# Tail transposes issued at once, ScalarE's casts kept behind a pair's second exponential, in the last turns of a fused attention and gated-linear kernel

## The chip, the cores and the metric

The kernel runs on one core of one Trainium2 chip. The metric is the device time of one execution, in microseconds. Five engines work side by side: TensorE (PE in the profile, its weight loads as PEld), VectorE (DVE), ScalarE (ACT), GpSimd (POOL) and SyncE (SP), which issues the transfers. Each engine takes its own instructions in the order in which the program lists them, and semaphores order the engines among each other.

## The reference

```python
x = A_x                                     # 1 x 2048 x 512
g = sigmoid((x * gate_w).sum(-1, keepdims=True))
# A: 32 heads of 16, causal, window 256
q, k, v = split(x @ wqkv)
s = (q @ k.T) * 16 ** -0.5                  # masked to 0 <= i - j < 256
a = (softmax(s) @ v) @ wo
# B: F = 1376
b = (sigmoid(x @ w_gate) * (x @ w_up)) @ w_down
return g * a + (1 - g) * b
```

All tensors are float32. Most matmuls are done in a rounded format three times over, as high part times high part, high times low and low times high, so that a "split" of a tile is a ScalarE cast (the high part) followed by a VectorE subtraction (the low part).

## The kernel before

**Stages.** The sequence of 2048 is cut into 16 blocks of 128 and the heads into 8 groups of 4. A prologue loads and splits x and projects the first values, queries and keys. Then one long loop runs over `u` from 0 to 139. A turn `u` handles one block of one head group for the scores (`s_part`, TensorE into the PSUM tile `s`, then a VectorE reduction to row maxima, L321) and, nine turns later, for the transposed scores (`st_part`, TensorE into `st`, then ScalarE's exponential into `pt`, L366). GpSimd masks `pt`, and every second turn TensorE multiplies two such blocks with the values into `pv` (L394). `s` and `st` have two PSUM banks each. After the loop comes the down projection (tiles `pd`, `hb`) with the output projection (`pa`).

**Fill work.** Between the score matmuls of each head `hh`, the loop puts matmuls of other products: projections of later head groups, the gate and up products (`gu`), and at the end 16 tail groups (`tp`), each of which holds what is left of F and the gate vector for one block of 128 positions. The generator `turns()` hands them out in portions of three steps, and each step is two matmuls on the two row halves of TensorE, where the second half runs 18 steps behind the first. So a group of 12 steps takes 30 steps from its first to its last matmul, and three groups are open in the three banks of the tag `misc`. When a group has ended, its bank must be emptied before the group three later can start: `gu` and projections by a ScalarE copy, tail groups by `tail_post`, a VectorE transpose (L525), a one-column copy (L526), and an entry in `later` for the store to `tail_scratch`.

**The order of the small work.** It is set by hand with two lists. `acts` holds closures that issue ScalarE work, and one is taken per head after the exponential; `behind` holds the VectorE work that follows them, and one is taken per head just before. `acts` gets the emptying of a finished group (put first), the copy of `pv` to `ob` (`o_take`, L410, put first, whose clearing of `pv`, L411, goes first into `behind`), and the splits of weights: `split_d` (L121, low part L122) and `wo_split` (L634, L635). `later` is sent on SyncE's queue at the start of the next turn.

**The last turns.** The scores end with u = 127, and the transposed scores go on to u = 136. From u = 128 on, the portions come in pairs, at the second and the fourth head of a turn. So TensorE does two `st` tiles, twelve `tp` matmuls, two `st` tiles, twelve `tp` matmuls in a turn, and `pv` at the start of each even turn. Here "pair" is two `st` tiles and the twelve matmuls behind them. Below, a pair's exponentials are called first and second.

```python
if t >= SHIFT and (t - SHIFT) % k3 == k3 - 1:          # L623, in turns()
    _, after, post = groups[(t - SHIFT) // k3]
    acts.insert(0, lambda after=after, post=post: (post(), after()))
...
    if behind:                                         # L792, per head
        behind.pop(0)()
    if acts:
        acts.pop(0)()
```

Of the kernel before, what the change touches and what calls it, by code (L numbers as in the profile page):

```python
# [24 lines left out]
NB = T // P  # L25
# [30 lines left out]
def gated_mix_kernel(  # L56
# [49 lines left out]
    NU = NG * NB  # L106
# [22 lines left out]
    with ExitStack() as actx:  # L129
# [175 lines left out]
        def s_part(u, hh):  # L305
            g, i = divmod(u, NB)
            s = g * NC + i // 4
            if i % 4 == 0 and hh == 0:
                mxs[s] = spool.tile([P, HG, 4], F32, tag="mx", name=f"mx{s}")
            k0 = max(0, i - 2)  # L310
            tag = "st" if u < LAG and hh >= 2 else "s"
            pt = ps.tile([P, 3 * P], F32, tag=tag, name=f"s{u}_{hh}", bufs=2)
            lhsT = blk(g, i, hh, 0)
            for k, e in pieces(g, k0, i + 1):
                mm(  # L315
                    pt[:, (k - k0) * P:(e - k0) * P], lhsT, blk(g, k, hh, 1, e - k),
                    start=k == k0, stop=e == i + 1, skip_group_check=True,
                )
            n = (i + 1 - k0) * P
            junk = spool.tile([P, 3 * P], F32, tag="junk", name=f"junk{u}_{hh}", bufs=1)  # L320
            nc.vector.tensor_tensor_reduce(  # L321
                junk[:, 0:n], pt[:, 0:n], mask[:, 3 * P - n:], scale=1.0, scalar=NEG,
                op0=ALU.add, op1=ALU.max, accum_out=mxs[s][:, hh, i % 4:i % 4 + 1],
            )
# [28 lines left out]
        def st_part(u, hh):  # L353
            g, j = divmod(u, NB)
            if u not in pts:
                pts[u] = ppool.tile([P, HG, 3 * P], F32, tag="pt", name=f"pt{u}", bufs=3)
            pt = ps.tile([P, 3 * P], F32, tag="st", name=f"st{u}_{hh}", bufs=2)
            lhsT = blk(g, j, hh, 1)
            last = min(NB, j + 3)
            for q, e in pieces(g, j, last):  # L360
                mm(  # L361
                    pt[:, (q - j) * P:(e - j) * P], lhsT, blk(g, q, hh, 0, e - q),
                    start=q == j, stop=e == last, skip_group_check=True,
                )
            n = (last - j) * P
            nc.scalar.activation(pts[u][:, hh, 0:n], pt[:, 0:n], AF.Exp, scale=SCALE)  # L366
# [15 lines left out]
        acts = []  # L382
        obs = {}

        def pv_part(u):
            g, j = divmod(u, NB)
            p = pts.pop(u)
            last = min(NB, j + 3)
            q = j
            while q < last:  # L390
                e = min(last, (q // 4 + 1) * 4)
                for hh in range(HG):
                    h = g * HG + hh
                    mm(  # L394
                        pv[32 * hh:32 * hh + 32, (q % 4) * P:(q % 4 + e - q) * P],
                        V[:, j, h * VW:h * VW + 32],
                        p[:, hh, (q - j) * P:(e - j) * P],
                        start=False, stop=True, skip_group_check=True,
                        tile_position=(0, 32 * hh),
                    )  # L400
                q = e
            if j % 2 == 1:
                acts.insert(0, lambda: o_take(g * NC + j // 4, j // 2 % 2))
# [71 lines left out]
        def gu_mm(f, c, w, k, half=None):  # L475
            if (f, c, w) not in gp:
                gp[f, c, w] = ps.tile([P, CH], F32, tag="misc", name=f"gu{f}_{c}_{w}", bufs=3)
            group_mm(gp[f, c, w], gv[:, 0, w], gv[:, 1, w], c, k, half)
# [35 lines left out]
        def tail_mm(b, k, half=None):  # L514
            if b not in tp:
                tp[b] = ps.tile([P, CH], F32, tag="misc", name=f"tp{b}", bufs=3)
            d, w = divmod(k, 3)
            r = slice(0, P) if half is None else slice(64 * half, 64 * half + 64)
            mm(tp[b][:, 0:TW], (xl if w == 1 else xh)[r, d, b * P:(b + 1) * P], tw[d][int(w == 2)][r, 0:TW],  # L519
               start=k == 0 and half != 1, stop=k == 3 * ND - 1 and half != 0,  # L520
               skip_group_check=half is not None)

        def tail_post(b):
            t = cpool.tile([P, CH], F32, tag="sp", name=f"tt{b}", bufs=4)
            nc.vector.transpose(t[:, 0:2 * TF], tp[b][:, 0:2 * TF])  # L525
            nc.vector.tensor_copy(gsum[:, b:b + 1], tp.pop(b)[:, 2 * TF:2 * TF + 1])  # L526
            later.append((tail_d[b], t[:, 0:2 * TF]))
# [38 lines left out]
        def proj_slot(s, k, half):  # L566
            g, c = divmod(s, NC)
            d, w = divmod(k, 2) if k < 2 * ND else (k - 2 * ND, 2)
            r = slice(64 * half, 64 * half + 64)
            mm(pair_of_banks(f"ph{s}")[half], wq[g][int(w == 2)][r, d], (xl if w == 1 else xh)[r, d, c * CH:(c + 1) * CH],  # L570
               start=k == 0, stop=k == 3 * ND - 1)

        def proj_sum(s):
            lower, upper = halves.pop(f"ph{s}")
            t = cpool.tile([P, CH], F32, tag="sp", name=f"psum{s}", bufs=4)
            nc.scalar.copy(t, lower)
            pj[s] = t
            behind.append(lambda: nc.vector.tensor_tensor(t, upper, t, op=ALU.add))
            soon.append(lambda: proj_post(s))
# [6 lines left out]
                lambda k, h=None, a=(f, c, w): gu_mm(*a, k, h),  # L586
# [2 lines left out]
            )  # L589
            for f in range(NFM) for w in range(2) for c in range(NC)  # L590
        ] + [
            (lambda k, h=None, b=b: tail_mm(b, k, h), lambda: None, lambda b=b: tail_post(b)) for b in range(NB)
        ]
        work = []
        going = []
# [4 lines left out]
        def run_first(n):  # L600
            for _ in range(n):
                if not going:
                    going.append([0, *(work or first).pop(0)])
                k, step, post = going[0]
                for half in range(2):
                    step(k, half)
                going[0][0] += 1
                if k + 1 == 3 * ND:
                    going.clear()
                    post()  # L610

        def turns():
            k3 = 3 * ND
            groups = []
            for t in range(n_rest * k3 + SHIFT):
                if t and t % GAP == 0:
                    yield
                if t % k3 == 0 and len(groups) < n_rest:
                    groups.append((work or rest).pop(0))
                for half, v in enumerate((t, t - SHIFT)):  # L620
                    if 0 <= v < n_rest * k3:
                        groups[v // k3][0](v % k3, half)
                if t >= SHIFT and (t - SHIFT) % k3 == k3 - 1:  # L623
                    _, after, post = groups[(t - SHIFT) // k3]
                    acts.insert(0, lambda after=after, post=post: (post(), after()))

        def slot(h, d, c):
            return (xh, xl)[h][:, d, c * CH:(c + 1) * CH]
# [8 lines left out]
        def flush(acts):  # L637
            while acts:
                acts.pop(0)()
# [86 lines left out]
        HLOAD = N - 2 * AHEAD  # L726
        done = 0
        slots = turns()
        sdma = []
        wo_raw = []  # L730

        for u in range(N):
# [35 lines left out]
            if s4 is not None:  # L768
                if u < LAG:
                    first.insert(0, (  # L770
                        lambda k, h, s4=s4: proj_slot(s4, k, h), lambda s4=s4: proj_sum(s4)))
# [4 lines left out]
            for hh in range(HG):  # L776
                if hh == 0 and u % 2 == 0:
                    for w in (u - PVLAG - 1, u - PVLAG):
                        if 0 <= w < NU:
                            pv_part(w)  # L780
                if u < NU:
                    s_part(u, hh)
                if 0 <= u - LAG < NU:
                    st_part(u - LAG, hh ^ 1 if u < NU else hh)
                if u < LAG:
                    flush(behind)
                    if hh % 2 == 1:
                        upto = n_first * (2 * u + 1 + hh // 2) // (2 * LAG)
                        run_first(upto - done)
                        done = upto  # L790
                else:
                    if behind:  # L792
                        behind.pop(0)()
                    if acts:
                        acts.pop(0)()
                if u >= LAG and (hh < HG - 1 or u % 2 == 0 if u < NU else hh % 2 == 1):
                    next(slots, None)
                    if u >= NU:
                        next(slots, None)
# [87 lines left out]
        for n, (c, f) in enumerate(steps):  # L887
# [42 lines left out]
            for t in range(4):  # L930
                b = 4 * c + t
# [60 lines left out]
```

## Time and profile before

| | |
|---|---|
| time, median of 3 runs | 745.94 us (745.91 to 746.12) |
| span of the profiled execution | 743.8 us |
| TensorE busy | 737.1 us (99%) |
| VectorE, ScalarE, GpSimd busy | 504.5, 432.3, 171.7 us |
| mean granted TensorE clock | 0.999 |
| tail groups' matmuls | from 507.4 to 576 us of the span |
| turns u = 128 to 137 | about 532.6 to 570 us |

The profile page gives the span of the profiled execution; its own time is not listed beside it, and the three timed runs lie 2.1 us above the span. Times inside the trace are counted from the span's start. In a row of the timeline stand start, duration, engine, line, operation, output<-inputs, shape and count, and in brackets how long the engine had been idle and what ended that. A matmul's end is modelled, so its starts say more than its duration.

### The profile page before, as it was taken

To read this page: it belongs to the slowest core of one execution; us is meant where nothing else is said; L and a number is where in the kernel's file an instruction comes from. 1 tells how busy PE (TensorE), PEld (TensorE's weight loads), DVE (VectorE), ACT (ScalarE), POOL (GpSimd) and SP (SyncE) were. 2 spreads that over 40 slices of the span, in tenths; PEclk is the share of its full clock that TensorE was granted. 3 is DMA by queue.
4 is the path that set the end of the run, shared out by engine and by line. 5 is a ranking of instruction groups with operands and counts; after the bars stand their busy time and mean duration, and the time that the engine had idled before them with its cause. 6 is when DMAs were issued, how large, how long until landed. Compare 5 with 4: busy or idle time off the path is not lost.

```text
span 743.8 us, 17724 instructions
## 1 busy us (share of the span) xinstructions
PE 737.1 (99%) x6310; PEld 585.2 (79%) x6310; DVE 504.5 (68%) x1518; ACT 432.3 (58%) x921; POOL 171.7 (23%) x256
## 2 busy tenths in 40 slices
PE   8999999999999999999999999999999999999997
PEld 7888777887777877778787787778777878787886
DVE  5368767766776766776677676677745685848573
ACT  6423676666676667666667666766655573625341
POOL 7000333233233233323323333232331000000000
PEclk9999999999999999999999999999999999999999
DMA  8341434435434453443543426553367878869561
GB/s 302 102 115 34 103 97 118 127 91 160 125 103 119 120 152 109 120 113 110 153 117 99 126 69 174 151 144 116 92 239 206 233 190 212 196 169 227 148 136 58
DMA packets 94321, 103.66 MB, mean 139 GB/s; under 512 B 44926, under 2 KB 57214, under 8 KB 94232
## 3 DMA queue, kind: packets, MB, share of 16 engines
q1 hardware_dynamic: 94232, 102.53, 49.9%
q8 instruction: 49, 0.80, 0.5%
q14 instruction: 40, 0.33, 0.2%
HBM read 45.32 MB, written 31.99 MB: 104 GB/s over the span
## 4 chain that ended last, share of the span: by engine, by line
PE 97%; DVE 1%; DMA 1%; issue 0%; ACT 0%; SPq 0%; POOL 0%; DVEq 0%; POOLq 0%
PE gu L247 28%; PE pv L394 12%; PE pj L247 11%; PE s L315 7%; PE st L361 5%; PE tp L519 5%; PE pd L78 5%; PE pd L80 5%; PE pd L79 5%; PE vh L556 3%; PE pa L78 2%; PE pa L79 2%; PE pa L80 2%; PE vps L79 1%; PE vps L78 1%; PE vps L80 1%
## 5 line engine op out<-in xcount | busy, mean ns | idle before, releaser
L321 DVE CUSTOM_DVE_ANT_0 junk<-s,mask 128x384 f32<-128x384 f32 (+2 forms) x512 | 271.8, 531 | 126.3 <-PE s L315 69.7
L366 ACT ACTIVATE pt<-st 128x384 f32<-128x384 f32 (+2 forms) x512 | 241.6, 474 | 169.9 <-PE st L361 65.3
L247 PE MATMUL gu<-xh,w 64*128 64x512 f32 x1152 | 295.1, 392 | 0.0
L247 PE MATMUL gu<-xl,w 64*128 64x512 f32 x576 | 190.5, 392 | 0.0
L371 POOL TENSOR_SCALAR_AFFINE_SELECT pt<-pt 128x512 f32<-128x512 f32 x128 | 87.7, 685 | 377.2 <-ACT pt L366 377.2
L247 PEld LDWEIGHTS gu<-xh,w 64*128 64x128 f32 x1152 | 160.6, 184 | 14.1
L361 PE MATMUL st<-ring 64*128 64x384 f32 (+2 forms) x536 | 170.1, 332 | 0.2 <-ACT pt L366 0.2
L315 PE MATMUL s<-ring 64*128 64x384 f32 (+2 forms) x536 | 166.6, 329 | 0.4 <-DVE mx L321 0.4
L315 PEld LDWEIGHTS s<-ring 64*128 64x128 f32 x536 | 95.3, 184 | 37.3 <-DVE nm L331 12.5
L361 PEld LDWEIGHTS st<-ring 64*128 64x128 f32 x536 | 97.0, 184 | 11.2 <-issue 2.7
L247 PEld LDWEIGHTS gu<-xl,w 64*128 64x128 f32 x576 | 90.6, 185 | 3.8
L394 PE MATMUL pv<-pt,V 128*32 128x384 f32 (+2 forms) x1408 | 91.0, 388 | 0.0
L247 PE MATMUL pj<-xh,wqh 64*128 64x512 f32 (+1 forms) x228 | 88.6, 395 | 0.4 <-ACT xh L74 0.4
L247 PE MATMUL pj<-xl,wqh 64*128 64x512 f32 (+1 forms) x228 | 88.2, 393 | 0.2 <-DVE xl L75 0.2
L376 POOL TENSOR_SCALAR_AFFINE_SELECT pt<-pt 128x512 f32<-128x512 f32 x112 | 74.4, 664 | 0.0
L247 PE MATMUL pj<-xh,wql 64*128 64x512 f32 (+1 forms) x228 | 69.9, 392 | 0.0
L394 PEld LDWEIGHTS pv<-pt,V 128*32 128x32 f32 x1408 | 37.2, 109 | 35.6 <-issue 29.5
L78 PE MATMUL pd<-ring,hb 128*128 128x512 f32 x160 | 63.0, 394 | 0.0
L80 PE MATMUL pd<-ring,hb 128*128 128x512 f32 x160 | 62.8, 392 | 0.0
L79 PE MATMUL pd<-ring,hb 128*128 128x512 f32 x160 | 62.3, 390 | 0.0
L74 ACT CAST hb<-V 128x512 fp32r<-128x512 f32 x40 | 24.9, 623 | 53.0 <-DVE V L700 51.3
L247 PEld LDWEIGHTS pj<-xh,wqh 64*128 64x128 f32 (+1 forms) x228 | 41.7, 185 | 3.4 <-ACT xh L74 0.9
(122 smaller groups left out, 1145.0 us busy)
## 6 DMA issues: line engine op xcount, KB each, us to landing
gu_scratch<-sp SPq DMA_DIRECT2D x72, 256.0 KB
V<-gu_scratch SPq DMA_DIRECT2D x36, 512.0 KB
ring<-sh SPq DMA_DIRECT2D x128, 128.0 KB
ring<-sl SPq DMA_DIRECT2D x64, 128.0 KB
guraw<-in_wgu_dram SPq DMA_DIRECT2D x18, 256.0 KB
V<-in_xT_dram SPq DMA_DIRECT2D x16, 256.0 KB
oT_scratch<-ob SPq DMA_DIRECT2D x128, 32.0 KB
xl<-oT_scratch SPq DMA_DIRECT2D x16, 256.0 KB
```

The lines of the kernel that those rows point to most:

```text
L78: mm(ps, lh, rh, start=first, stop=False)
L79: mm(ps, lh, rl, start=False, stop=False)
L80: mm(ps, ll, rh, start=False, stop=last)
L247: mm(pt, (wl if w == 2 else wh)[r, d], (xl if w == 1 else xh)[r, d, c * CH:(c + 1) * CH], start=k == 0 and half != 1, stop=k == 3 * ND - 1 ...
L315: mm(pt[:, (k - k0) * P:(e - k0) * P], lhsT, blk(g, k, hh, 1, e - k), start=k == k0, stop=e == i + 1, skip_group_check=True,)
L321: nc.vector.tensor_tensor_reduce(junk[:, 0:n], pt[:, 0:n], mask[:, 3 * P - n:], scale=1.0, scalar=NEG, op0=ALU.add, op1=ALU.max, accum_out ...
L361: mm(pt[:, (q - j) * P:(e - j) * P], lhsT, blk(g, q, hh, 0, e - q), start=q == j, stop=e == last, skip_group_check=True,)
L366: nc.scalar.activation(pts[u][:, hh, 0:n], pt[:, 0:n], AF.Exp, scale=SCALE)
L371: nc.gpsimd.affine_select(p[:, :, 0:P], p[:, :, 0:P], pattern=[[0, HG], [1, P]], compare_op=ALU.is_ge, fill=0.0, base=0, channel_multiplie ...
L376: nc.gpsimd.affine_select(p[:, :, 2 * P:], p[:, :, 2 * P:], pattern=[[0, HG], [-1, P]], compare_op=ALU.is_gt, fill=0.0, base=0, channel_mu ...
L394: mm(pv[32 * hh:32 * hh + 32, (q % 4) * P:(q % 4 + e - q) * P], V[:, j, h * VW:h * VW + 32], p[:, hh, (q - j) * P:(e - j) * P], start=Fals ...
L519: mm(tp[b][:, 0:TW], (xl if w == 1 else xh)[r, d, b * P:(b + 1) * P], tw[d][int(w == 2)][r, 0:TW], start=k == 0 and half != 1, stop=k == 3 ...
```

## The change

A tail group gets `None` in place of its empty "after" step, and `turns()` takes that as a sign to issue the transpose, the one-column copy and the entry in `later` at once, where the group's last matmul is issued, and not through `acts`. And from u = 128 on (`u >= NU`), an entry of `acts` is taken only at the second and fourth head, that is behind the second exponential of each pair, where before one was taken behind every exponential.

```diff
-            (lambda k, h=None, b=b: tail_mm(b, k, h), lambda: None, lambda b=b: tail_post(b)) for b in range(NB)
+            (lambda k, h=None, b=b: tail_mm(b, k, h), None, lambda b=b: tail_post(b)) for b in range(NB)
...
                     _, after, post = groups[(t - SHIFT) // k3]
-                    acts.insert(0, lambda after=after, post=post: (post(), after()))
+                    if after is None:
+                        post()
+                    else:
+                        acts.insert(0, lambda after=after, post=post: (post(), after()))
...
-                    if acts:
+                    if acts and (u < NU or hh % 2 == 1):
                         acts.pop(0)()
```

TensorE's and GpSimd's programs stay as they were, apart from line numbers (three more behind L625). Before u = 124 nothing moves on any engine.

The first place is VectorE's program at the border of turns 125 and 126. The rows named `junk` are the reductions of score tiles `s`, each followed by the row that stores its maximum; `tp_8743` is a tail group.

```order
 L321 ISA junk_3_8909,mx_8860<-s_3_8907,mask 128x384
 L321 ISA mx_8860 128x1
-L321 ISA junk_0_8925,mx_8860<-s_0_8923,mask 128x384
-L321 ISA mx_8860 128x1
-L525 STREAM_TRANSPOSE tt_8931<-tp_8743 128x448
+L525 STREAM_TRANSPOSE tt_8920<-tp_8743 128x448
 L526 COPY gsum<-tp_8743 128x1
-L321 ISA junk_1_8942,mx_8860<-s_1_8940,mask 128x384
-L321 ISA mx_8860 128x1
-L321 ISA junk_2_8956,mx_8860<-s_2_8954,mask 128x384
+L321 ISA junk_0_8929,mx_8860<-s_0_8927,mask 128x384
+L321 ISA mx_8860 128x1
```

The transpose now stands ahead of the reduction of turn 126's first score tile, and not behind it. The same happens to the other three tail groups that end before u = 128.

The second place is VectorE's program in turn 130. `tp_9156` (before) and `tp_9155` (now) are the same tail group, L122 is the low part of a weight split whose cast is in ScalarE's program below, and L713 is L716 in the changed kernel.

```order
-L713 RECIPROCAL sm_9125<-sm_9125 128x128
+L716 RECIPROCAL sm_9125<-sm_9125 128x128
+L525 STREAM_TRANSPOSE tt_9282<-tp_9155 128x448
+L526 COPY gsum<-tp_9155 128x1
 L411 MEMSET pv 128x256
 L122 TENSOR_TENSOR ring<-wdraw_9132,ring 128x512
-L525 STREAM_TRANSPOSE tt_9288<-tp_9156 128x448
-L526 COPY gsum<-tp_9156 128x1
```

The transpose and its copy are now ahead of the clearing of `pv` and of the low part, both of which wait for ScalarE; before they were behind both.

The third place is ScalarE's program in the same turn 130, with the four exponentials of `st_0` to `st_3`, the copy of `pv` and a cast of the down projection's weights.

```order
 L366 ACTIVATE pt_9260<-st_0_9261 128x384
-L410 COPY ob_9149<-pv 128x256
-L366 ACTIVATE pt_9260<-st_1_9266 128x384
+L366 ACTIVATE pt_9260<-st_1_9265 128x384
+L410 COPY ob_9153<-pv 128x256
+L366 ACTIVATE pt_9260<-st_2_9285 128x384
+L366 ACTIVATE pt_9260<-st_3_9289 128x384
 L121 CAST ring<-wdraw_9132 128x512
-L366 ACTIVATE pt_9260<-st_2_9284 128x384
-L366 ACTIVATE pt_9260<-st_3_9291 128x384
```

The copy has gone from behind the first exponential to behind the second, and the cast from behind the second to behind the fourth. Turns 128 to 136 are changed in this manner throughout. On SyncE's queue, one store to `tail_scratch` moves ahead of the load L347, and the rest keeps its order.

## The prediction, written before the changed kernel ran

> **What bounds the kernel now.** I read the page first, then the busy time by stretches, then the timeline from 515 to 594 us row by row.
>
> ```profile
> PE 737.1 (99%) x6310; PEld 585.2 (79%) x6310; DVE 504.5 (68%) x1518; ACT 432.3 (58%) x921; POOL 171.7 (23%) x256
> ...
> PE 97%; DVE 1%; DMA 1%; issue 0%; ACT 0%; SPq 0%; POOL 0%; DVEq 0%; POOLq 0%
> ```
>
> TensorE is busy for 99% of the span and is 97% of the chain that ended last. Only its waits can go, and since a matmul's end is modelled, a wait shows in the distance between starts rather than as idle time. So I looked for starts further apart than their like. This is the stretch of turns 130 and 131:
>
> ```profile
> 542.14 0.45 PE L361 MATMUL st<-ring 64*128 64x384 f32 x2
> ...
> 543.07 0.37 ACT L410 COPY ob<-pv 128x256 f32<-128x256 f32 x1
> ...
> 543.32 0.51 ACT L366 ACTIVATE pt<-st 128x384 f32<-128x384 f32 x1
> ...
> 543.64 0.67 PE L361 MATMUL st<-ring 64*128 64x384 f32 x2
> 543.70 0.63 ACT L121 CAST ring<-wdraw 128x512 fp32r<-128x512 f32 x1
> ...
> 544.36 0.69 DVE L122 TENSOR_TENSOR ring<-wdraw,ring 128x512 fp32r<-128x512 f32 x1 [0.53 <-ACT ring L121]
> ...
> 544.97 0.65 DVE L525 STREAM_TRANSPOSE tt<-tp 128x448 f32<-128x448 f32 x1
> ...
> 545.22 0.49 PE L361 MATMUL st<-ring 64*128 64x384 f32 x2
> 545.54 0.12 DVE L526 COPY gsum<-tp 128x1 f32<-128x1 f32 x1
> 545.66 0.87 ACT L366 ACTIVATE pt<-st 128x384 f32<-128x384 f32 x2 [0.56 <-PE st L361]
> 545.81 0.44 PE L519 MATMUL tp<-tail_wqh,xh 64*128 64x450 f32 x1
> ...
> 547.12 0.36 PE L361 MATMUL st<-ring 64*128 64x384 f32 x2
> 547.30 0.36 PE L519 MATMUL tp<-tail_hb,xh 64*128 64x450 f32 x1
> ...
> 547.49 0.87 ACT L366 ACTIVATE pt<-st 128x384 f32<-128x384 f32 x2 [0.96 <-PE st L361]
> ...
> 548.64 1.50 PE L394 MATMUL pv<-pt,V 128*32 128x384 f32 x16
> ```
>
> Two kinds of wait can be seen. *The bank of a tail group*: behind the `st` tiles at 547.12 the next tail matmul starts 0.18 us later, behind those at 545.22 it starts 0.59 us later. The copy that frees the old group's bank ends at 545.66, and the matmul starts 0.15 us after that. The transpose was late because VectorE takes its program in order, and ahead of it stood the low part L122, which waited for the cast L121. *The bank of a second `st` tile*: ScalarE's copy of `pv` stands between the two exponentials of the pair at 542.14, so the second ends at 543.83. The second tile of the next pair, which needs that bank, cannot start at 543.64 beside the first, and its row is 0.67 us long instead of 0.36. Turn 129 shows this alone:
>
> ```profile
> 537.17 0.34 PE L361 MATMUL st<-ring 64*128 64x384 f32 x1
> ...
> 538.57 0.33 PE L361 MATMUL st<-ring 64*128 64x384 f32 x1
> ...
> 539.11 0.44 PE L361 MATMUL st<-ring 64*128 64x384 f32 x1 [0.17 <-ACT pt L366]
> ```
>
> From 537.17 to 538.57, 1.40 us, is a pair without a wait, and the one behind it is held at 539.11 by an exponential that had a cast ahead of it.
>
> **The change part by part.** *Turns 128 to 136.* I cost them by blocks of two turns, from one `pv` to the next:
>
> ```profile
> 532.59 1.50 PE L394 MATMUL pv<-pt,V 128*32 128x384 f32 x16
> ...
> 540.70 1.51 PE L394 MATMUL pv<-pt,V 128*32 128x256 f32 x32
> ...
> 556.63 1.51 PE L394 MATMUL pv<-pt,V 128*32 128x256 f32 x32
> ...
> 559.58 0.67 PE L361 MATMUL st<-ring 64*128 64x384 f32 x2
> ...
> 561.15 0.43 PE L361 MATMUL st<-ring 64*128 64x256 f32 x2
> ...
> 562.83 0.38 PE L361 MATMUL st<-ring 64*128 64x256 f32 x1
> ```
>
> Without waits a block is `pv` 1.44 (540.70 to 542.14), a first pair 1.50 (542.14 to 543.64), two pairs of 1.40, and a last pair up to `pv` of 1.52 (547.12 to 548.64): 7.26 us. The blocks took 8.11 (532.59 to 540.70), 7.94 (to 548.64) and 7.99 us (to 556.63), so 0.85, 0.68 and 0.73 too long. In the fourth block the pair of 559.58 took 1.57 to 561.15, 0.17 too long, and in turn 135, where only one row half is left, 562.83 is a tile held by an exponential behind a cast (its two tiles and six tail matmuls of 0.20 would need 1.5 us, and it took 1.68): 0.17 more. Sum 2.60 us.
>
> Does all of it go? The transpose now needs only the end of its group. In turn 130 the group's last matmuls are those just ahead of 543.64; with the 0.36 of a tail matmul's row they end at about 543.8, and with 0.65 and 0.12 for transpose and copy the bank is free at about 544.6. It is wanted at 545.4. For the exponentials the margin is thin. The pair at 545.22 has two exponentials with nothing between them: they start 0.44 behind the tiles and end at 546.53, 1.31 after, against the 1.40 at which the second tile of the next pair comes. The cast behind them takes its place at about 1.20 (0.44 and twice 0.38, the distance from the exponential of 543.32 to the instruction behind it), where the engine is otherwise free until the next pair's exponential at 1.40 + 0.37 (547.12 to 547.49) = 1.77. In turn 130 the exponential that follows the cast of 543.70 starts at 544.21, 0.51 later, so the cast holds the engine to 1.71. It fits with 0.06 to spare. The Trainium skill, "ScalarE: Activation LUTs", section "What ACT_TABLE_LOAD costs", gives 186 ns plus 0.833 ns an element for such an instruction, and 93 ns of overlap between neighbours. By it two exponentials take 0.92 us rather than the 0.87 of the row, a pair would end at 1.36 instead of 1.31, still before 1.40, and the sum stays; the measured row decides. Bounds: from 0 gained (every cast holds the next pair as long as it now holds its own) to 2.60. I take 2.60, as the nearest rows fit.
>
> *Turns 124 to 127.* Here the transpose is moved ahead of a score reduction.
>
> ```profile
> 522.48 0.56 DVE L321 CUSTOM_DVE_ANT_0 junk<-s,mask 128x384 f32<-128x384 f32 x1
> ...
> 522.97 0.65 DVE L525 STREAM_TRANSPOSE tt<-tp 128x448 f32<-128x448 f32 x1
> ...
> 523.34 0.33 PE L361 MATMUL st<-ring 64*128 64x384 f32 x1
> 523.53 0.12 DVE L526 COPY gsum<-tp 128x1 f32<-128x1 f32 x1
> ...
> 523.80 0.44 PE L519 MATMUL tp<-tail_wqh,xh 64*128 64x450 f32 x1
> ...
> 528.71 0.33 PE L315 MATMUL s<-ring 64*128 64x384 f32 x1
> 528.84 0.12 DVE L526 COPY gsum<-tp 128x1 f32<-128x1 f32 x1
> ...
> 529.10 0.44 PE L519 MATMUL tp<-tail_wqh,xh 64*128 64x450 f32 x1
> ```
>
> Two of the four groups make TensorE wait here, again 0.14 to 0.15 us behind the end of the copy: 523.80 − 523.34 − 0.18 = 0.28, and 529.10 − 528.71 − 0.18 = 0.21; each adds 0.08 because the first row behind a wait is 0.44 long instead of 0.36. At the first place the reduction of 522.48 now comes about 0.6 later, since the transpose takes its place, and a score tile that reuses its bank waits till about 523.55; so nearly as much is lost as is won. Ends: −0.3 (a loss) to 0.36; I take 0.1. At the second the reduction behind the transpose ends at about 528.5, just before its bank is wanted at 528.71: 0 to 0.29, and I take 0.29.
>
> *What is moved besides.* The stores to `tail_scratch` come earlier with their transposes. The copy of `pv`, its clearing and the casts come up to one pair later, 1.4 us; the next `pv` is a turn away, and the split weights are read only in the down projection. They cost nothing while they end before that. A weight load on SyncE's queue that reuses a split's buffer may wait up to 1 us longer; the queue has idle time there.
>
> *Does it reach the end?* Behind the loop TensorE again runs without gaps, so a gain is kept if the down projection's inputs move with it. Their margin is small:
>
> ```profile
> 568.82 0.34 SPq L289 DMA_DIRECT2D tail_scratch<-tt  x1
> ...
> 581.49 0.45 SPq L647 DMA_DIRECT2D V<-gu_scratch  x1
> ...
> 587.22 0.63 ACT L699 ACTIVATE V<-V 128x512 f32<-128x512 f32 x1 [2.90 <-DMA V<-gu_scratch]
> ...
> 592.30 0.69 DVE L75 TENSOR_TENSOR hb<-V,hb 128x512 fp32r<-128x512 f32 x1
> ...
> 593.26 0.39 PE L80 MATMUL pd<-ring,hb 128*128 128x512 f32 x1
> ```
>
> ScalarE waits 2.90 us for the load issued at 581.49, and one step later VectorE ends the low part of `hb` at 592.99, only 0.27 us before TensorE reads it. But that load stands in a queue that from 568.82 on issues almost without a break, and that row waited for a transpose (line L525 of the last group) that the change brings forward. So I expect the load to be issued earlier by at least as much as TensorE comes.
>
> Sum: 2.60 + 0.1 + 0.29 = 2.99 us. The profiled span is 743.8, and the median of the runs 745.94 lies 2.1 above it; I leave that as it is. 745.94 − 2.99 = 742.95, so 743.0 us. A difference of 0.2%, 1.5 us, is about what a measurement can tell from none.
>
> **The rivals.** *The inputs of the down projection do not move* (about the same). If the loads are set by the transfers before them, TensorE waits there for all that it won beyond the 0.27 us: 745.94 − 0.27 = 745.7. For it speaks the 2.90 us row; against it, that this load is issued late and not merely served late. Chance 0.10.
>
> *The reductions give it back* (about the same). The Trainium skill, "PSUM — Partial Sum Buffer", section "Engine vs sequencer instructions", says that VectorE's and ScalarE's queues are strict first in, first out; the row of 544.36 ahead of that of 544.97 agrees. By that order four transposes with their copies, about 0.7 us each, stand ahead of score reductions. If TensorE waited for each in full, 2.8 us are lost, against 2.60 won from turn 128 on: 746.1. Against it: three of the four reductions have room, as worked out above. Chance 0.04.
>
> *The change does not do what it says*: TensorE waits for something else than the copy or the exponential. 745.9. The same 0.14 to 0.15 us behind three copies speaks against it. Chance 0.03.
>
> *A held queue* (slower). SyncE's queue issues in order, and its stores of `ob` now follow a copy that comes later.
>
> ```profile
> SPq L289 <- ACT ob L410: 4.6, 3, 3.5
> ```
>
> The longest such wait is 3.5 us. If one like it fell between 568.82 and 581.49, the load of 581.49 would be issued 3.5 us later than now, and TensorE, with its margin of 0.27, would end at 745.94 + 3.5 − 0.27 = 749.2. It decides from 1.8 us of lateness on (1.8 − 0.27 = 1.5). Against it: the last copy keeps its place behind the last `pv`. Chance 0.07.
>
> **How the numbers follow.** The forecast has 0.76, with its own range from 742.4 (no new wait in turns 124 to 127, and the longer first rows gone as well) to 744.4 (half the sum). The rest is 0.10, 0.04, 0.03 and 0.07. The range 742.4 to 745.3 holds the forecast and the half of the first rival in which part of the gain passes. Faster by over 0.2% is the forecast and a fifth of the first rival, 0.78; slower is the last rival, 0.07; within 0.2% is the remaining 0.15.
>
> **What would show it.** In the changed profile, blocks from `pv` to `pv` of about 7.3 us instead of 7.9 to 8.1; tail matmuls 0.18 behind the `st` tiles; second tiles beside the first; no wait in the rows of 523.80 and 529.10's like, but perhaps one in a score tile's; the first `pd` matmul some 3 us earlier than now; and steps 5 and 6 of the down projection without a wait. It is wrong if casts now push the next pair's exponentials so that blocks stay near 8 us, or if the won time is lost again behind 580 us.

## The result, and the profile after

The changed kernel took 743.13 us (median of 5 runs, 742.95 to 743.49), the kernel before 745.94 us beside it: a ratio of 0.9964, 95% interval 0.9953 to 0.9975, so 2.8 us faster. The profiled execution took 743.2 us with a span of 741.5, against a span of 743.8 before.

The page of the changed kernel, busy times and the chain that ended last:

```profile
PE 735.4 (99%) x6310; PEld 586.3 (79%) x6310; DVE 505.3 (68%) x1518; ACT 432.2 (58%) x921; POOL 173.9 (23%) x256
...
PE 96%; DMA 2%; DVE 1%; issue 0%; ACT 0%; SPq 0%; DVEq 0%
```

TensorE is still the bound, and its busy time is 1.7 us shorter. Since no instruction of it was taken away, I take that for wait that a modelled end had counted as work. The blocks tell more. TensorE's timeline of the changed kernel, the `pv` rows from turn 124 on, the first matmul of the down projection and the last of the kernel:

```profile
517.32 1.50 PE L394 MATMUL pv<-pt,V 128*32 128x384 f32 x16
...
532.37 1.50 PE L394 MATMUL pv<-pt,V 128*32 128x384 f32 x16
...
539.78 1.51 PE L394 MATMUL pv<-pt,V 128*32 128x256 f32 x32
...
547.59 1.50 PE L394 MATMUL pv<-pt,V 128*32 128x384 f32 x16
...
554.89 1.51 PE L394 MATMUL pv<-pt,V 128*32 128x256 f32 x32
...
562.08 1.50 PE L394 MATMUL pv<-pt,V 128*32 128x384 f32 x16
...
573.58 0.50 PE L78 MATMUL pd<-ring,hb 128*128 128x512 f32 x1
...
737.20 0.39 PE L80 MATMUL pa<-xh,xl 128*128 128x512 f32 x1
```

and the same of the kernel before, where the prediction did not show them:

```profile
517.07 1.50 PE L394 MATMUL pv<-pt,V 128*32 128x384 f32 x16
...
564.37 1.50 PE L394 MATMUL pv<-pt,V 128*32 128x384 f32 x16
...
575.91 0.50 PE L78 MATMUL pd<-ring,hb 128*128 128x512 f32 x1
...
739.55 0.39 PE L80 MATMUL pa<-xh,xl 128*128 128x512 f32 x1
```

What lies ahead of the first row is the same program in all kernels here, yet the row stands between 516.5 and 518.1 us in their profiles. So I count from it. To the last matmul it is 222.48 us before and 219.88 after, 2.60 less. The blocks of turns 128 to 135 take 7.41, 7.81, 7.30 and 7.19 us where they took 8.11, 7.94, 7.99 and 7.74. One of them, the second, has hardly gained.

The waits that the prediction named are gone. In turns 130 and 131 of the changed kernel:

```profile
542.72 0.40 PE L361 MATMUL st<-ring 64*128 64x384 f32 x2
...
543.50 0.12 DVE L526 COPY gsum<-tp 128x1 f32<-128x1 f32 x1
...
543.85 0.62 ACT L121 CAST ring<-wdraw 128x512 fp32r<-128x512 f32 x1
...
544.55 0.45 PE L361 MATMUL st<-ring 64*128 64x384 f32 x2 [0.21 <-ACT ring L121]
544.81 0.36 PE L519 MATMUL tp<-tail_wqh,xh 64*128 64x450 f32 x1
...
546.03 0.40 PE L361 MATMUL st<-ring 64*128 64x384 f32 x2
```

The second tiles stand beside the first (0.40 for two, where 543.64 showed 0.67), and VectorE frees a group's bank at 543.62, about a microsecond before TensorE wants it. But the tiles of 544.55 are late: 1.83 us after those of 542.72, where a pair takes 1.40 (the last pair of the block, 546.03 to 547.59, takes 1.56, near the 1.52 that it took before). The row blames the cast of 543.85. But these tiles read other parts of `ring` than that cast writes.

### The profile page after: what moved, and what is told of

It is laid out like the page before. It is cut to its first block, busy times and chain, and to the rows that moved or that the text cites. A ratio compares the mean times of both kernels' runs of the same rounds, so it can differ in the third digit from the quotient of the medians.

```text
span 741.5 us, 17721 instructions
## 1 busy us (share of the span) xinstructions
PE 735.4 (99%) x6310; PEld 586.3 (79%) x6310; DVE 505.3 (68%) x1518; ACT 432.2 (58%) x921; POOL 173.9 (23%) x256
## 4 chain that ended last, share of the span: by engine, by line
PE 96%; DMA 2%; DVE 1%; issue 0%; ACT 0%; SPq 0%; DVEq 0%
PE gu L247 28%; PE pv L394 12%; PE pj L247 11%; PE s L315 8%; PE tp L519 5%; PE st L361 5%; PE pd L80 5%; PE pd L78 5%; PE pd L79 5%; PE vh L556 3%; PE pa L78 2%; PE pa L79 2%; PE pa L80 2%; DMA V<-in_xT_dram 2%; PE vps L78 1%; PE vps L79 1%
## 5 line engine op out<-in xcount | busy, mean ns | idle before, releaser
L371 POOL TENSOR_SCALAR_AFFINE_SELECT pt<-pt 128x512 f32<-128x512 f32 x128 | 88.1, 688 | 372.4 <-ACT pt L366 372.4
L376 POOL TENSOR_SCALAR_AFFINE_SELECT pt<-pt 128x512 f32<-128x512 f32 x112 | 76.2, 680 | 0.0
L247 PEld LDWEIGHTS pj<-xl,wqh 64*128 64x128 f32 (+1 forms) x228 | 41.7, 185 | 3.4 <-DVE xl L75 1.4
```

Of the source, the lines that this page charges most:

```text
L247: mm(pt, (wl if w == 2 else wh)[r, d], (xl if w == 1 else xh)[r, d, c * CH:(c + 1) * CH], start=k == 0 and half != 1, stop=k == 3 * ND - 1 ...
L371: nc.gpsimd.affine_select(p[:, :, 0:P], p[:, :, 0:P], pattern=[[0, HG], [1, P]], compare_op=ALU.is_ge, fill=0.0, base=0, channel_multiplie ...
L376: nc.gpsimd.affine_select(p[:, :, 2 * P:], p[:, :, 2 * P:], pattern=[[0, HG], [-1, P]], compare_op=ALU.is_gt, fill=0.0, base=0, channel_mu ...
```

## The experiments

All times are medians; every kernel ran beside the kernel before.

**Each half alone.** The change has two halves: (a), the transposes at once, and (b), the casts kept behind the second exponential. `e1` keeps (a) and drops (b):

```diff
-                    if acts and (u < NU or hh % 2 == 1):
+                    if acts:
```

> Half (a) alone: a tail group's transpose is put into VectorE's program at once, ScalarE's casts stay where they were, also between the two exponentials of a pair. If the two kinds of wait add up (each half takes its own): the waits for a tail group's bank go, 0.41 and 0.43 us in the second and third block and some 0.33 in turns 124 to 127, so 1.2 us less than the kernel before, 744.8, and the second tiles stay late, with the first block at 8.0 us or more. If each wait is the cover of the other, so that TensorE is held by whichever ends last: under 0.4 us less, 745.6 or more.

It took 745.16 us, ratio 0.9988 (0.9979 to 0.9996): 0.9 us faster. Its blocks are 8.14, 7.55, 8.01 and 7.73 us. Only the second gains, 0.39; the third, where I expected 0.43, gains nothing, because with its bank free a second tile waits instead (the timeline of `e1`, where the second of two tiles waits for the exponential of 554.65 behind the cast, so that the row is 0.93 us long):

```profile
554.14 0.61 ACT L121 CAST ring<-wdraw 128x512 fp32r<-128x512 f32 x1
554.65 0.49 ACT L366 ACTIVATE pt<-st 128x384 f32<-128x384 f32 x1
554.71 0.93 PE L361 MATMUL st<-ring 64*128 64x384 f32 x2
...
555.19 0.18 PEld L361 LDWEIGHTS st<-ring 64*128 64x128 f32 x1 [0.50 <-ACT pt L366]
```

Turns 124 to 127 take 15.01 us instead of 15.52. So neither expectation held as a whole: the waits add up in one block and cover each other in the next. `e2` is the kernel before with (b) alone, so that the transposes go through the list:

```diff
-                    if acts:
+                    if acts and (u < NU or hh % 2 == 1):
```

> Half (b) alone: ScalarE's casts and copies from turn 128 on only behind the second exponential of a pair; the transposes still go through the same list, so they too are issued only there. If the waits add up: the second tiles' waits go, about 0.7 us in the first block, 0.27 and 0.30 in the second and third, 0.3 in the fourth, so about 1.5 us less, 744.4, while the 0.4 us waits for a tail group's bank and the two waits in turns 124 to 127 stay. If the later transposes hold the banks longer than the casts held the exponentials: no gain, 745.5 or more, and waits for the bank in every block.

It took 749.94 us, ratio 1.0057 (1.0044 to 1.0071), 3.9 us *slower*. Neither theory had that, and the loop does not show it either. Its `pv` rows and those behind them:

```profile
516.57 1.50 PE L394 MATMUL pv<-pt,V 128*32 128x384 f32 x16
...
532.07 1.50 PE L394 MATMUL pv<-pt,V 128*32 128x384 f32 x16
...
561.32 1.50 PE L394 MATMUL pv<-pt,V 128*32 128x384 f32 x16
...
574.88 0.65 PE L78 MATMUL pd<-ring,hb 128*128 128x512 f32 x1 [1.95 <-ACT hb L74]
...
592.30 0.50 PE L78 MATMUL pd<-ring,hb 128*128 128x512 f32 x1 [1.83 <-ACT hb L74]
...
742.26 0.39 PE L80 MATMUL pa<-xh,xl 128*128 128x512 f32 x1
```

Turns 128 to 135 take 29.25 us instead of 31.78: 2.53 won, with no wait for a tail group's bank left. (b) alone does all of the loop's work there. Then TensorE waits twice in the down projection, and from 516.57 to the last matmul it is 225.69 us, 3.21 more than before. ScalarE and VectorE of `e2` show two reasons:

```profile
568.23 1.14 ACT L634 CAST xh<-woraw 128x512 fp32r<-128x512 f32 x2
569.27 1.66 ACT L121 CAST ring<-wdraw 128x512 fp32r<-128x512 f32 x3
...
571.69 1.89 DVE L122 TENSOR_TENSOR ring<-wdraw,ring 128x512 fp32r<-128x512 f32 x3
573.50 0.68 DVE L700 TENSOR_TENSOR V<-V 128x512 f32<-128x512 f32 x1
...
590.19 0.63 ACT L699 ACTIVATE V<-V 128x512 f32<-128x512 f32 x1 [6.92 <-DMA V<-gu_scratch]
```

The first wait is for work that has piled up. Five casts stand behind the last copy of `pv` where the changed kernel has two, and VectorE comes to the first product of the down projection (L700) only behind their low parts. Before these it was held 0.93 us by a late load, that of the sums. ScalarE itself waits for no load there. The second wait is for a load that ScalarE waits 6.92 us for, and that load is late on SyncE's queue. The queue's waits in `e2`, and the same line in the changed kernel (us in total, number of waits, the longest):

```profile
SPq L113 <- DVE ring L122: 8.5, 2, 6.0
```

```profile
SPq L113 <- DVE ring L122: 1.5, 2, 1.3
```

A weight load at line L113 needs a buffer that a cast and its low part L122 must first empty. It stood 6.0 us at the head of the queue, and with it every load and store behind it. The load for step 5 of the down projection (a step is twelve matmuls) left at 584.27, where the changed kernel's left at 578.41: counted from turn 124, 6.6 us later. My reading: from turn 128 on (b) takes one entry of the list in a pair, and a transpose that goes through the list takes the place of a cast. So the casts come late, at the end of the loop all at once, and both waits follow from that. `e7` tests it: (b) alone with the transposes as late as in `e2`, but in a list of their own. Against `e2`, with tail groups marked by `None` as in the changed kernel:

```diff
+        posts = []
...
-                    acts.insert(0, lambda after=after, post=post: (post(), after()))
+                    if after is None and u >= NU:
+                        posts.append(post)
+                    else:
+                        acts.insert(0, lambda after=after, post=post: (post(), after and after()))
...
+                    if posts and hh % 2 == 1:
+                        posts.pop(0)()
                     if acts and (u < NU or hh % 2 == 1):
...
             if u >= N - 2:
+                flush(posts)
                 flush(acts)
```

> Casts alone (the second half of the change), but with the tail groups' transposes from turn 128 on in a list of their own, of which one is taken behind each second exponential beside one cast, so that they take no cast's place; they are issued as late as with the casts alone. Theory: the casts alone lost their 2.6 us and 3.9 more because a transpose took a cast's place in the list, the casts of the weight loads' buffers came late, and SyncE's queue stood 6.0 us at a weight load (line L113) behind the low part L122, which held all loads of the down projection. With the places free the loop keeps its 2.6 us, that wait is under 1.5 us, and the time is about 743.4 (the changed kernel and the two waits of turns 124 to 127). Rival: it was the late transposes themselves, whose stores to tail_scratch the loads wait for; then it stays at 748 to 750.

It took 744.14 us, ratio 0.9971 (0.9959 to 0.9984). The wait at L113 is down to one of 1.1 us, TensorE no longer waits in the down projection, and the loop keeps what `e2` won: 532.99 to 562.38 is 29.39 us. The time is 0.7 us above the 743.4 expected, but 5.8 us less than `e2`, by nothing but the casts' places. The rival, late transposes, falls.

**The place of the casts.** `e5` is the changed kernel with `hh % 2 == 0`: as many casts, but between the two exponentials.

> The changed kernel with the other side of the pair: from turn 128 on ScalarE's casts and copies are taken only behind the first exponential of a pair, between the two, as many of them as in the changed kernel. Theory (place): a cast between the exponentials ends the second one 0.51 us later, 1.82 instead of 1.31 behind its tiles, later than the 1.40 at which the next pair's second tile wants the bank; blocks from pv to pv of 7.8 to 8.0 us where there are casts, time 745.0 to 745.5. Rival (number): what helped is only that no more than one cast is taken in a pair, and that no transpose stands behind the low part of a cast; then blocks of 7.3 and 743.1.

It took 744.91 us, just under the 745.0 expected, ratio 0.9984 (0.9975 to 0.9993), blocks 8.12, 7.75, 7.98 and 7.73. Its timeline has the old picture back:

```profile
542.52 0.37 ACT L410 COPY ob<-pv 128x256 f32<-128x256 f32 x1
...
542.77 0.51 ACT L366 ACTIVATE pt<-st 128x384 f32<-128x384 f32 x1
...
543.10 0.67 PE L361 MATMUL st<-ring 64*128 64x384 f32 x2
...
543.33 0.18 PEld L361 LDWEIGHTS st<-ring 64*128 64x128 f32 x1 [0.25 <-ACT pt L366]
```

The second exponential ends at 543.28, and the weights of the tile that reuses its bank go in only at 543.33. Place, not number, holds the tiles; the rival falls.

**Turns 124 to 127.** `e6` is the changed kernel with the transposes at once only from turn 128 on:

```diff
-                    if after is None:
+                    if after is None and u >= NU:
```

> The changed kernel with the transposes at once only from turn 128 on; those of turns 124 to 127 go through the list again. Theory: the waits of 0.2 to 0.3 us in turns 124 to 127 are back, so that the two blocks ahead of turn 128 take 7.7 and 7.8 us instead of 7.58 and 7.47, about 0.4 in sum; but turn 131 then comes 0.4 us later, and its wait for the maxima (0.49) all but vanishes, since their landing doesn't move: the second block takes 7.4, and the time is that of the changed kernel, 743.1 to 743.3. Rival: the maxima land later too, because the stores ahead of them do, and the 0.4 us are lost: 743.5.

743.86 us, above what either view expected, ratio 0.9963 (0.9950 to 0.9977), which the runs cannot tell from the changed kernel's 0.9964. In the profile, turns 124 to 127 take 7.72 and 7.79 us again, 0.46 more than with the change, the second block 7.59 instead of 7.81, and to the last matmul it is 220.20 us instead of 219.88. So half of the loss is given back in the second block, not all: the maxima landed 0.26 later as well, counted from turn 124. Two profiles of the changed kernel itself differ by 0.15 in that landing (27.10 us behind the row of turn 124 here, 26.95 in the one further down), so the size is rough. In the profile both views were half right.

**The second block.** Line L347 loads the last row maxima, which the tiles of turn 131 are the first to read. On SyncE's queue of the changed kernel it stands behind the 1 MB load of `wo`:

```profile
537.36 0.46 SPq L767 DMA_DIRECT2D woraw<-in_wo_dram  x1
537.91 0.45 SPq L289 DMA_DIRECT2D tail_scratch<-tt  x1
538.55 0.56 SPq L347 DMA_DIRECT2D ring<-max_scratch  x1
```

The trace's records of the semaphore that it raises end at 544.42, 5.87 us after its issue, and the late tiles start 0.13 us behind that. `e3` lets `wo` go one turn later, behind the maxima:

```diff
-WO = 128
+WO = 129
```

> The changed kernel, with the 1 MB load of wo (woraw) issued in turn 129 behind the load of the last row maxima (line L347) instead of in turn 128 ahead of it. Theory: the 0.4 us that the second block is too long in the changed kernel is the wait of turn 131's first tiles for that load, which lands at 544.4 in the profile's time, behind the 1 MB; it then lands before 542, the tiles start 0.4 us earlier, the block goes from 7.81 to about 7.4, and the time is 742.7, 0.4 under the changed kernel. Rival: the tiles waited for ScalarE, whose cast of line L121 ended last before them; then the block stays at 7.8 and the time at 743.1.

SyncE's queue and the tiles in `e3`:

```profile
538.15 0.56 SPq L347 DMA_DIRECT2D ring<-max_scratch  x1
538.77 0.43 SPq L767 DMA_DIRECT2D woraw<-in_wo_dram  x1
...
542.86 0.39 PE L361 MATMUL st<-ring 64*128 64x384 f32 x2
...
543.99 0.62 ACT L121 CAST ring<-wdraw 128x512 fp32r<-128x512 f32 x1
...
544.28 0.38 PE L361 MATMUL st<-ring 64*128 64x384 f32 x2
```

The maxima land at 541.63, 3.48 us after their issue. The tiles come 1.42 us behind the pair before, *while* the cast of 543.99 is still running, and carry no wait. The block takes 7.33 us, and from the first `pv` row to the last matmul it is 219.34 us, 0.54 less than in the changed kernel. The wait was the load's; the row's name for it was wrong. In the kernel before, the same edit:

> The kernel before, with the same move of the load of wo. Theory: in it turn 131 comes 0.7 us later, behind the landing of the maxima, so nothing waits for them and the time stays: 745.9, within 0.2. Rival: the order of these two loads is worth something by itself (for the tail stores or the weight loads behind them); then the time changes by 0.4 us or more here as well.

746.36 us, ratio 1.0004 (0.9995 to 1.0012): nothing. In the kernel before the maxima landed at 544.57 and the tiles came at 545.22, so they did not wait. The edit pays only after the change.

The median of `e3` was 743.16, no less than the changed kernel's. Both ran once more, side by side (the expectation says turn 122; the `pv` row meant is that of turn 124):

> The changed kernel with the maxima loaded ahead of wo, once more, side by side with the changed kernel itself. Its profile was 0.54 us shorter than the changed kernel's from turn 122 to the end, but the medians of the runs (743.16 and 743.13) did not show it. Theory: the 0.49 us of the wait are really won and reach the end; the profile is again 0.4 to 0.6 us shorter from the pv of turn 122 to the last instruction, and the median 0.2 to 0.8 us under the changed kernel's in the same series. Rival: it is lost again behind the loop; then both agree within 0.1 in the stretch to the end.

> The changed kernel as it is, for the comparison above. Theory: second block 7.8 us again, with the tiles of turn 131 starting 0.1 to 0.2 us behind the landing of the maxima; median 743.1 to 743.5.

743.09 us (ratio 0.9962, 0.9948 to 0.9976) against 743.84 (0.9967, 0.9957 to 0.9977). In the profiles 219.32 against 219.77 us to the last matmul, 0.45 less, and in the changed kernel again a landing at 544.13 with the tiles at 544.26. Two expectations for the changed kernel missed: its second block took 7.62 us and not 7.8, and its median lies above 743.1 to 743.5. So the half microsecond is real in the profile, and the run times lean the same way but do not separate the two. `e3` is the fastest version that ran, by an amount that only profiles show.

## Why the prediction was right, and where its sizes were off

743.0 us was forecast and 743.13 measured, within the range, with the mechanism that was named. Counted from turn 124, 2.99 us were expected and the profile shows 2.60. That the times agree to 0.13 us is partly luck: terms missed to both sides, and in the later series the same kernel took 743.84 us, 2.2 less than the kernel before beside it. Step by step:

*The blocks of turns 128 to 136: 2.60 expected, 2.07 measured* (31.78 to 29.71 us). The first and third blocks gave 0.70 and 0.69 for 0.85 and 0.73. The fourth gave 0.55 for 0.34. I had counted its waits from two places only, and the pair from 561.15 to 562.83, which I put at 1.5 us without its wait, takes 1.38 now. The second gave 0.13 for 0.68, and this is the step that failed: "Does all of it go?" asked after the bank and the exponentials, and not after the loads that the tiles read. By `e3` the same blocks take 29.24 us, a gain of 2.54. So the term was right for what it looked at, and 0.5 short for a wait that had been hidden behind the old ones.

*Two kinds of wait.* I had taken one for each half, as the expectations of `e1` and `e2` have it. That split did not hold. With (b) alone no wait for a bank is left in these blocks (`e2`, 2.53 of 2.60), for the low part L122 no longer stands ahead of a transpose with its cast still to come. With (a) alone they gain 0.35 (`e1`, 31.43 us).

*The thin margin of the exponentials held.* Two exponentials and a cast fit into a pair, and blocks of 7.3 us show it; `e5` shows what a misplaced cast costs.

*Turns 124 to 127: 0.39 expected, 0.47 measured* (15.52 to 15.05 us), with the score tile's wait in place of the bank's, as foreseen. The changed kernel's rows at the first place, where the tile starts 0.06 us behind the reduction:

```profile
523.12 0.54 DVE L321 CUSTOM_DVE_ANT_0 junk<-s,mask 128x384 f32<-128x384 f32 x1
...
523.60 0.08 DVE L321 DVE_READ_ACCUMULATOR2_ANT mx<- 128x1 f32 x1
...
523.74 0.44 PE L315 MATMUL s<-ring 64*128 64x384 f32 x1
```

*It reaches the end.* The loop gave 2.54, the last matmul 2.60. The first `pd` matmul came 2.58 us earlier, counted from turn 124, where I had said some 3. The load for step 5 was issued 3.08 us earlier in the profile (3.33 counted from turn 124), and ScalarE waits less for it:

```profile
578.41 0.45 SPq L650 DMA_DIRECT2D V<-gu_scratch  x1
...
583.80 0.63 ACT L702 ACTIVATE V<-V 128x512 f32<-128x512 f32 x1 [1.83 <-DMA V<-gu_scratch]
```

The low part of `hb` is now ready 1.5 us ahead of TensorE at steps 5 and 6, where it was 0.45 and 0.27 (0.9 and 0.6 in the second profile of the changed kernel). So the step held, and TensorE does not wait at steps 5 and 6. It was argued in one sentence, and most hung on it. With half of the change, the same end of the kernel lost everything: in `e2` 2.55 us were won by turn 136 and 5.8 lost behind it. The first rival, inputs that do not move, is what happened in `e1`'s profile, where TensorE waits at step 5 and of 0.86 us won by turn 136 0.19 are left at the last matmul. There the load of the sums was issued 3.14 us behind the store that it needs (575.92 to 579.06) instead of 2.02; the run times, 0.9 us better, say that this is not so in most runs: the profiled run was the slowest of the eleven. Why it waited there stays open.

*A held queue*, 0.07, slower. In the changed kernel the longest wait at L113 is 1.3 us, near the "up to 1 us longer". But a held queue is part of what made `e2` slow, at another line than I had named: not a store that waits for a copy, but a weight load that waits for a cast. Where I priced the copy's wait, I should have asked which casts are taken later when fewer are taken in a pair. (a) is what keeps that from happening, and this, not its earlier transposes, is its worth from turn 128 on: `e7` has late transposes and casts in time, and is within 0.3 us of the changed kernel in the profile (29.39 against 29.71 us in the blocks; 220.02 against 219.88 us to the last matmul).

*The other two rivals* did not come. Turns 124 to 127 gained, so the reductions gave nothing back there; for "three of the four reductions have room" I had worked out only two places. And the waits went with the copies and the exponentials that were moved, so TensorE had waited for them.

## What to carry to other kernels

A list that is emptied one entry at a time is a resource: slowing it moves everything in it, so count its entries against its places, and follow the last one to the buffer that it frees and to the queue that waits for the buffer. When a wait goes, look for loads whose landing hardly moves, since the row that follows names only what ended last. And measure halves of a change from a common mark to the end: a half that wins in its own stage can lose the whole behind it.

## What the hardware showed that I had not expected

In `e2` the wait ahead of 574.88 cost more than its length. The matmuls behind it start 0.43 us apart, later 0.23. By stretches, with the granted clock in the column behind the engines:

```profile
core 0: us, PE busy (x) PEld busy (x) DVE busy (x) ACT busy (x) POOL busy (x), PEclk, DMA share, GB/s
560.00:572.50 12.50, 12.50 (x85) 9.72 (x84) 7.45 (x16) 7.36 (x18) 1.27 (x2) 1.00 0.60 184
...
574.90:578.30 3.40, 3.40 (x8) 2.48 (x9) 2.71 (x5) 1.69 (x4) 0.00 (x0) 0.52 0.74 161
578.40:590.00 11.60, 11.60 (x52) 9.54 (x51) 4.12 (x9) 2.75 (x5) 0.00 (x0) 1.00 0.70 193
...
592.30:600.00 7.70, 7.64 (x32) 5.88 (x33) 7.24 (x15) 5.94 (x10) 0.00 (x0) 1.00 0.79 250
```

After 1.95 us of idle time (row 574.88) the granted clock was 0.52 for 3.4 us, which put the third matmul of step 1 1.3 us further behind the first matmul than it was before (4.91 us from 574.88 to 579.79, against 3.61). It was not this one execution: the mean granted clock is 0.997 or 0.998 in all six runs of `e2`, and 0.999 or 1.000 in those of the kernel before beside it. The second wait, nearly as long (1.83 us, row 592.30), left the clock at 1.00. The Trainium skill, "TensorE: Matmul & The Clock Gate", section "What's actually happening", describes a gate that halves the clock after an idle window of about 3.4 us that runs freely, and opens it after a busy window as long; half the clock and the 3.4 us of recovery agree with the row, but here a pause shorter than the window was enough once, and once not.

A matmul that waited for the load of the maxima started 0.13 to 0.14 us behind its landing in all four profiles in which it did wait (544.42 to 544.55, 544.13 to 544.26, 544.23 to 544.37 in `e6`, 544.69 to 544.82 in `e7`). And a load of 16 KB took 5.87 us behind one of 1 MB on the same queue, and 3.48 us ahead of it; over all profiles it was 5.4 to 5.9 us in the eight with the first order and 3.4 to 3.8 us in the three with the second.
